# Attention and two feed-forward blocks on one core: the last product by quarters, PSUM by single banks, a new order of attention

## The chip, the cores and the metric

One core of a Trainium2 chip runs the whole program. The metric is the device time of one execution in microseconds (us), the median of several. The engines are TensorE (PE), VectorE (DVE), ScalarE (ACT), GpSimd (POOL) and SyncE (SP, which issues most DMAs); each takes its own instructions in the program's order.

## The reference

```python
# q, k, v: (2, 12, 448, 64), causal attention
scores = scale * q @ k.T                     # masked above the diagonal
attn = exp(scores - max); attn /= attn.sum() + 1e-9
x = (attn @ v)                               # (896, 768), tokens x heads*64
h = x @ w_in                                 # w_in (768, 2048)
y = (relu(h) ** 2) @ w_out                   # (896, 768)
z = maximum(maximum(y @ w1, y @ w2), y @ w3) # each w (768, 768)
out = z @ moe2_w_out                         # (896, 768)
```

## The kernel before

Everything is held transposed (features on partitions, tokens along the free axis), 448 tokens (one batch) to a matmul. Weights arrive in double precision: `Weight` (L131) loads raw words (L143), and DVE and ACT decode them in steps `clip`, `scale`, `shift`, `join`, `sign`, then split them into a high part (ACT, `act_hi`, L125) and a low part (DVE, `dve_lo`, L128). Activations are split likewise, and each product is three matmuls: high x high, high x low, low x high (`group`, L328).

**Attention** handles 12 pairs of heads. The steps of a pair are scores (`s`, L226, PE), masked minimum (`m`, L237, DVE), exponential (`e`, L246, ACT), reciprocal (`r`, DVE), normalising (`n`, L258, POOL), transposes (`g`, L266, PE), placing them in SBUF (`h`, L290, DVE for group 0, else ACT), weighted sums with v (`w`, L299, PE), and the split of the result (`xh` on ACT, `xl` on DVE). The hand-written list `ORDER` (L23) gives the order of all steps, `s4.0` being scores 4 of pair 0; each engine keeps that order. q and k of pair i + 3 are loaded at `s0.i`, v of pair i + 2 at `w0.i`. Decoding of the first `w_in` blocks (`wload`, `wc` to `wl`) and the product of block 0 for the first batch (`p0.f0` to `gl.f0`) stand in the list too. Eight warm-up matmuls of 448 columns on a zero operand come first (L446 to L449). PSUM is a pool `psa`: four `sc` banks, three `pt`, one `pv`.

**The main loop** starts when that pool is closed and pool `psb` (four accumulators of two banks, one bank for each batch) takes its place. The rounds of `front` (L489: block 1, the second batch's half of block 0, then blocks 2 to 15) make 36 matmuls each (18 for the half), with relu (L363), square (L366) and split; then `w_out` (L497, 18 rounds), then the stage with w1, w2 and w3 (L517): for each of six blocks f three rounds, copy to `m`, two maxima (L527), split into `zh` and `zl`. `decode` (L421) does, in one round, the low part of the weight two places ahead in the line of weights and all other steps of the one three places ahead, with the evacuation of the round in between; block f of the last weight (`wo`) stands behind w1, w2, w3 of f in that line.

**The last product** (L535) goes over seven row tiles of 128 tokens: 36 matmuls of 384 columns each (six f, three parts, two halves; the seventh tile is cut 480 and 288), then ACT copies the first half, DVE the second (L557, L559), and SP sends the tile out.

Of the kernel before, what the change touches and what calls it, by code (L numbers as in the profile page):

```python
# [15 lines left out]
WARM = 8  # L16
PR, PT, SC, VP = 2, 3, 4, 1
# [6 lines left out]
wload.f0 wload.f1 s4.0 m4.0 m5.0 e4.0 e5.0 s6.0 m6.0 e6.0 s2.0 m2.0 m3.0 e2.0 e3.0 r0.0 n6.0 n5.0  # L24
n4.0 s0.0 m0.0 m1.0 e0.0 e1.0 s4.1 m4.1 m5.1 e4.1 e5.1 r1.0 n3.0 n2.0 s6.1 m6.1 e6.1 r2.0 n1.0
n0.0 g3.0 h3.0 s2.1 m2.1 m3.1 e2.1 e3.1 g0.0 h0.0 r0.1 n6.1 n5.1 n4.1 s0.1 m0.1 m1.1 e0.1 e1.1
s4.2 r1.1 n3.1 n2.1 g1.0 h1.0 r2.1 n1.1 n0.1 g2.0 h2.0 m4.2 m5.2 e4.2 e5.2 g3.1 h3.1 s6.2 m6.2
e6.2 g0.1 h0.1 s2.2 m2.2 m3.2 e2.2 e3.2 r0.2 n6.2 n5.2 n4.2 w0.0 w1.0 w2.0 w3.0 xh.0 s0.2 m0.2
m1.2 e0.2 e1.2 xl.0 s4.3 g1.1 h1.1 g2.1 h2.1 m4.3 m5.3 e4.3 e5.3 r1.2 n3.2 n2.2 r2.2 n1.2 n0.2
s6.3 m6.3 e6.3 g3.2 h3.2 g0.2 h0.2 s2.3 m2.3 m3.3 e2.3 e3.3 w0.1 w1.1 w2.1 w3.1 xh.1 r0.3 n6.3  # L30
n5.3 n4.3 s0.3 m0.3 m1.3 e0.3 e1.3 xl.1 s4.4 r1.3 n3.3 n2.3 g1.2 h1.2 g2.2 h2.2 m4.4 m5.4 e4.4
e5.4 r2.3 n1.3 n0.3 g3.3 h3.3 s6.4 m6.4 e6.4 g0.3 h0.3 s2.4 m2.4 m3.4 e2.4 e3.4 r0.4 n6.4 n5.4
n4.4 w0.2 w1.2 w2.2 w3.2 xh.2 s0.4 m0.4 m1.4 e0.4 e1.4 xl.2 s4.5 g1.3 h1.3 g2.3 h2.3 m4.5 m5.5
e4.5 e5.5 r1.4 n3.4 n2.4 s6.5 m6.5 e6.5 r2.4 n1.4 n0.4 g3.4 h3.4 g0.4 h0.4 s2.5 m2.5 m3.5 e2.5
e3.5 r0.5 n6.5 n5.5 n4.5 w0.3 w1.3 w2.3 w3.3 xh.3 s0.5 m0.5 m1.5 e0.5 e1.5 xl.3 s4.6 r1.5 n3.5
n2.5 g1.4 h1.4 r2.5 n1.5 n0.5 g2.4 h2.4 m4.6 m5.6 e4.6 e5.6 g3.5 h3.5 s6.6 m6.6 e6.6 g0.5 h0.5
s2.6 m2.6 m3.6 e2.6 e3.6 r0.6 n6.6 n5.6 n4.6 w0.4 w1.4 w2.4 w3.4 xh.4 s0.6 m0.6 m1.6 e0.6 e1.6
xl.4 s4.7 g1.5 h1.5 g2.5 h2.5 m4.7 m5.7 e4.7 e5.7 r1.6 n3.6 n2.6 r2.6 n1.6 n0.6 g3.6 h3.6 s6.7
m6.7 e6.7 g0.6 h0.6 s2.7 m2.7 m3.7 e2.7 e3.7 w0.5 w1.5 w2.5 w3.5 xh.5 r0.7 n6.7 n5.7 n4.7 s0.7
m0.7 m1.7 e0.7 e1.7 xl.5 s4.8 g1.6 h1.6 r1.7 n3.7 n2.7 g2.6 h2.6 m4.8 m5.8 e4.8 e5.8 r2.7 n1.7  # L40
n0.7 g3.7 h3.7 s6.8 m6.8 e6.8 g0.7 h0.7 s2.8 m2.8 m3.8 e2.8 e3.8 w0.6 w1.6 w2.6 w3.6 xh.6 wc.f0
# [19 lines left out]
def tile_attention_moe_moe(  # L61
# [25 lines left out]
    nc = tc.nc  # L87
# [43 lines left out]
    class Weight:  # L131
# [19 lines left out]
        def clip(self):  # L151
            self.t = wp.tile(self.shape, F32, tag="wd", name="wd", bufs=2)
# [36 lines left out]


# [12 lines left out]
    class Pair:  # L203
# [124 lines left out]
    def group(acc, w, kcs, cs, x, tks, first=True, last=True):  # L328

        for a, kc in enumerate(kcs):  # L330
            wh, wl = w(kc)
            for n in range(3):
                for i, tk in enumerate(tks):
# [3 lines left out]
                        acc[:, i, :S], ww[:, cs], xx[:, tk],  # L337
# [9 lines left out]
    def moe_in(psp, w, g, bs):  # L347

        nb = len(bs)
        shape = [P, 1, 512] if psp is psa else [P, B, 512]  # L350
        acc = psp.tile(shape, F32, tag="pt" if psp is psa else "acc", name="acc", bufs=PT if psp is psa else None)
# [40 lines left out]
    front = [*range(FILL, FILL + 1), *range(FILL), *range(FILL + 1, KFF)]  # L392
# [46 lines left out]
    with tc.tile_pool(name="ga", bufs=1) as ga:  # L439
        with (  # L440
            tc.tile_pool(name="att", bufs=2) as att,
            tc.tile_pool(name="psa", bufs=2, space=bass.MemoryType.PSUM) as psa,
        ):
            prs = [att.tile([P, offs[-1]], F32, name=f"pr{n}", bufs=1) for n in range(PR)]
            warm = tp.tile([P, B, S], FR, tag="r", name="warm")
            nc.vector.memset(warm.bitcast(F32), 0.0)  # L446
            idle = psa.tile([P, S], F32, tag="pt", name="idle", bufs=PT)
            for _ in range(WARM):
                nc.tensor.matmul(idle, warm[:, 0, :P], warm[:, 1], start=True, stop=True)  # L449
# [7 lines left out]
            for f in range(FILL + EARLY):  # L457
                w = blocks_in[f]
                e = dict(
                    wload=load_next, wc=w.clip, ws=w.scale, w1=w.shift, w2=w.join, w3=w.sign, wh=w.high_part,  # L460
                    wl=w.low_part,
                )
                if f < FILL:
                    def first(f=f):
                        todo.update({
                            f"{n}.f{f}": step for n, step in
                            moe_in(psa, blocks_in[f].hl, g_tiles(ga, f, [0]), [0]).items()
                        })
# [18 lines left out]
        psb = ctx.enter_context(tc.tile_pool(name="psb", bufs=4, space=bass.MemoryType.PSUM))  # L487
        with tc.tile_pool(name="gb", bufs=1) as gb:
            for f in front:  # L489
                bs = both if f >= FILL else both[1:]  # L490
                e = moe_in(psb, blocks_in[f].hl, g_tiles(gb, f, bs), bs)
# [5 lines left out]
            for m in range(KDM):  # L497
                acc = psb.tile([P, B, 512], F32, tag="acc", name="acc")
                for n, w in enumerate(blocks_out[m]):
# [7 lines left out]
                        lambda: [act_hi(yh[b][:, m], acc[:, b, :S]) for b in range(B)],  # L507
                        lambda: [dve_lo(yl[b][:, m], acc[:, b, :S], yh[b][:, m]) for b in range(B)],
# [6 lines left out]
    zh = zp.tile([P, KF2, NT], FR, name="zh")  # L515
    zl = zp.tile([P, KF2, NT], FR, name="zl")
    for f in range(KF2):  # L517
        m = None
        for n, w in enumerate(blocks_max[f]):
            acc = psb.tile([P, B, 512], F32, tag="acc", name="acc")  # L520
            group(acc, blocks(*w.hl), range(KDM), slice(0, P), y, [every] * B)
            a = acc[:, :, :S]
            if n == 0:
                m = tp.tile([P, B, S], F32, tag="r", name="m")
                decode([lambda: nc.scalar.copy(m, a)])
                continue
# [83 lines left out]
```

## Time and profile before

| | us |
|---|---|
| median of 3 runs | 500.53 (500.27 to 500.68) |
| the profiled execution | 500.39 |
| its span, first to last instruction | 498.5 |
| busy in the span: PE, DVE, ACT, POOL | 489.9, 337.3, 212.9, 45.0 |

A row of a timeline or group names the line of the kernel, the engine, the operation, output<-inputs by the program's names with their shapes, and a count; what stands in brackets is the time for which the engine stood idle ahead of it and what ended that. PEld is TensorE's weight load, which runs beside the matmuls. Ends of matmuls are modelled, so a busy PE need not be PE at its peak.

### The profile page before, as it was taken

How to read it: one execution, taken by the hardware profiler on the slowest of the kernel's cores; microseconds unless marked ns; L12 is line 12 of the kernel's file. 1: busy time of each engine (PE TensorE's matmuls, PEld its weight loads, DVE VectorE, ACT ScalarE, POOL GpSimd, SP SyncE). 2: the span in 40 equal slices, each digit the busy share in tenths (PEclk: the TensorE clock that was granted, in tenths of full speed). 3: DMA queues.
4: the chain of work that ended last, by engine and by line, in shares of the span. 5: the costliest groups of instructions: out<-in, count | busy, mean ns of one | idle time of the engine just before them, and what ended most of it. 6: DMA issues, size and time to landing. Idle time of an engine off the chain costs nothing.

```text
span 498.5 us, 6849 instructions
## 1 busy us (share of the span) xinstructions
PE 489.9 (98%) x2612; PEld 432.7 (87%) x2612; DVE 337.3 (68%) x626; ACT 212.9 (43%) x410; POOL 45.0 (9%) x97
## 2 busy tenths in 40 slices
PE   8999998899999999999999999999999999999996
PEld 5666666899999999999999999999999999999996
DVE  4877888688877787848448457467887979852000
ACT  4999995454445445433123223233433434321000
POOL 3655554000000000000000000000000000000000
PEclk9999999999999999999999999999999999999999
DMA  8433313344324323333333243233445335300111
GB/s 297 152 123 121 124 43 83 108 128 125 95 97 128 117 75 104 126 106 121 108 110 106 81 151 121 69 126 128 136 131 177 128 126 190 126 2 32 64 63 64
DMA packets 46464, 56.28 MB, mean 113 GB/s; under 512 B 1632, under 2 KB 41824, under 8 KB 46432
## 3 DMA queue, kind: packets, MB, share of 16 engines
q1 hardware_dynamic: 46288, 55.61, 34.5%
q8 instruction: 21, 0.34, 0.3%
q10 hardware_dynamic: 144, 0.23, 0.1%
q14 instruction: 11, 0.09, 0.1%
HBM read 53.08 MB, written 2.75 MB: 112 GB/s over the span
## 4 chain that ended last, share of the span: by engine, by line
PE 97%; DVE 2%; ACT 0%; POOLq 0%; issue 0%; POOL 0%
PE acc L336 73%; PE acc L546 9%; PE sc L226 6%; PE ptp L266 4%; PE pv L299 3%; PE idle L449 1%; POOLq L606 0%; DVE wd L167 0%; DVE wd L174 0%; DVE xl L128 0%; DVE pr L237 0%; DVE wd L163 0%; DVE warm L446 0%; DVE ph L290 0%; DVE r L366 0%
## 5 line engine op out<-in xcount | busy, mean ns | idle before, releaser
L125 ACT CAST wh<-wd 128x768 fp32r<-128x768 f32 (+1 forms) x52 | 42.2, 812 | 122.7 <-DVE wd L174 122.7
L336 PE MATMUL acc<-yl,wh 128*128 128x448 f32 x216 | 61.4, 365 | 0.0
L336 PE MATMUL acc<-yh,wh 128*128 128x448 f32 x216 | 61.3, 365 | 0.0
L336 PE MATMUL acc<-yh,wl 128*128 128x448 f32 x216 | 61.3, 365 | 0.0
L336 PE MATMUL acc<-xh,wh 128*128 128x448 f32 x192 | 55.7, 366 | 1.3 <-DVE xl L128 1.3
L159 ACT ACTIVATE wd<-wd 128x768 f32<-128x768 f32 (+1 forms) x58 | 47.8, 823 | 18.8 <-DVE wd L153 18.5
L167 DVE SCALAR_TENSOR_TENSOR wd<-wr,wd 128x768 int32<-128x768 int32 (+1 forms) x58 | 54.3, 936 | 2.0
L174 DVE SCALAR_TENSOR_TENSOR wd<-wr,wd 128x768 int32<-128x768 int32 (+1 forms) x58 | 54.2, 935 | 2.0
L128 DVE TENSOR_TENSOR wl<-wd,wh 128x768 fp32r<-128x768 f32 (+1 forms) x52 | 48.1, 925 | 10.9 <-ACT wh L125 10.7
L336 PE MATMUL acc<-xl,wh 128*128 128x448 f32 x192 | 55.5, 365 | 0.0
L336 PE MATMUL acc<-xh,wl 128*128 128x448 f32 x192 | 55.5, 365 | 0.0
L336 PE MATMUL acc<-gh,wh 128*128 128x448 f32 x192 | 54.5, 365 | 0.0
L336 PE MATMUL acc<-gh,wl 128*128 128x448 f32 x192 | 54.5, 365 | 0.0
L336 PE MATMUL acc<-gl,wh 128*128 128x448 f32 x192 | 54.5, 365 | 0.0
L246 ACT ACTIVATE pr<-pr,st 128x384 f32<-128x384 f32 (+3 forms) x84 | 43.9, 527 | 6.6 <-DVE st L237 6.3
L258 POOL TENSOR_SCALAR pr<-pr,st 128x384 f32<-128x384 f32 (+3 forms) x84 | 42.6, 526 | 36.3 <-DVE st L254 11.2
L237 DVE CUSTOM_DVE_ANT_0 pr<-sc,mask 128x384 f32<-128x384 f32 (+3 forms) x84 | 34.5, 447 | 15.9 <-PE sc L226 12.3
L336 PEld LDWEIGHTS acc<-yh,wl 128*128 128x128 f32 x216 | 40.6, 188 | 3.2
L336 PEld LDWEIGHTS acc<-yh,wh 128*128 128x128 f32 x216 | 40.6, 188 | 3.2
L336 PEld LDWEIGHTS acc<-yl,wh 128*128 128x128 f32 x216 | 40.6, 188 | 3.2
L336 PEld LDWEIGHTS acc<-xh,wh 128*128 128x128 f32 x192 | 36.0, 188 | 4.2 <-DVE xl L128 1.4
L336 PEld LDWEIGHTS acc<-xh,wl 128*128 128x128 f32 x192 | 36.1, 188 | 2.9
(93 smaller groups left out, 688.1 us busy)
## 6 DMA issues: line engine op xcount, KB each, us to landing
wr<-in_moe_w_out SPq DMA_DIRECT2D x18, 768.0 KB, 4.3
wr<-in_moe_w SPq DMA_DIRECT2D x18, 768.0 KB, 4.3
wr<-in_moe_w_in SPq DMA_DIRECT2D x16, 768.0 KB, 4.7
q<-in_q SPq DMA_DIRECT2D x12, 256.0 KB, 2.7
v<-in_v SPq DMA_DIRECT2D x12, 256.0 KB, 3.6
wr<-in_moe_w_out SPq DMA_DIRECT2D x6, 512.0 KB, 3.7
k<-in_k SPq DMA_DIRECT2D x11, 224.0 KB, 2.8
out<-o SPq DMA_DIRECT2D x6, 384.0 KB, 2.3
```

The lines of the kernel that those rows point to most:

```text
L125: nc.scalar.copy(hi, src)
L128: nc.vector.tensor_tensor(out=lo, in0=src, in1=hi.bitcast(F32), op=ALU.subtract)
L159: nc.scalar.activation(self.t, self.t, ACTF.Copy, scale=2.0 ** -112)
L167: nc.vector.scalar_tensor_tensor(out=ti, in0=self.low, scalar=29, in1=ti, op0=ALU.logical_shift_right, op1=ALU.bitwise_or,)
L174: nc.vector.scalar_tensor_tensor(out=ti, in0=self.high, scalar=SIGN, in1=ti, op0=ALU.bitwise_and, op1=ALU.bitwise_or)
L226: nc.tensor.matmul(sc[:, :keys[w]], self.n["q"][r, w // 2 * P:(w // 2 + 1) * P], self.n["k"][r, :keys[w]], start=True, stop=True,)
L237: nc.vector.tensor_tensor_reduce(out=self.pr[:, offs[u]:offs[u] + n], in0=self.sc[u][:, :n], in1=mask[:, mask.shape[1] - n:], scale=-SCALE ...
L246: nc.scalar.activation(sl, sl, ACTF.Exp, bias=self.st[:, 0, u:u + 1], scale=-1.0, accum_out=self.st[:, 1, u:u + 1],)
L258: nc.gpsimd.tensor_scalar(sl, sl, self.st[:, 2, u:u + 1], 1.0, op0=ALU.mult, op1=ALU.mult)
L266: nc.tensor.transpose(pt[:, i], self.pr[:, offs[u] + kc * P:offs[u] + (kc + 1) * P], ident)
L336: nc.tensor.matmul(acc[:, i, :S], ww[:, cs], xx[:, tk], start=first and a == 0 and n == 0, stop=last and a == len(kcs) - 1 and n == 2,)
L546: nc.tensor.matmul(acc[:, i, :cols[i].stop - cols[i].start], zz[:, f, tk], ww[:, 0, cols[i]], start=f == 0 and n == 0, stop=f == KF2 - 1 a ...
```

## The change

`ORDER` is written anew: pair 0 begins with its shortest scores, loads of weights come later, decoding of blocks 0 and 1 is spread otherwise, and the whole product of block 1 (`a0` to `a5`) and the second batch of block 0 (`b0` to `b5`) stand at its end. q and k of pair 0 are loaded in two pieces each. PSUM is eight tiles of one bank, given out in turn by kind (`bank`, `one`, `next_acc`), so relu, square, maximum and copy work on one batch at a time. The warm-up is 11 matmuls of 256 columns.

The last product takes the first 768 tokens in quarters of 384 tokens x 384 inner features x 384 columns: seven products of quarters and sums of quarters, in place of eight. Sums of quarters of z (`sums_z`) and of the weight (`sums_w`) are made on DVE, in place in the unsplit values, as soon as block f is there; block 5's after the stage. Four sums of each are then split in high and low (`z_sum`, `w_sum`). On PE come first the products that need no sums (`corner`, row tile 6 in `rest`, the second half of `corner`), then, for each of three row tiles, four products, two sums, and a fifth product onto the first one's bank. Results leave in halves of 384 columns.

```diff
-WARM = 8
-PR, PT, SC, VP = 2, 3, 4, 1
+WARM = 11
+PR = 2
...
+s0.0 m0.0 m1.0 e0.0 e1.0 r2.0 n1.0 s2.0 m2.0 m3.0 e2.0 e3.0 s4.0 m4.0 m5.0 e4.0 e5.0 n0.0 s6.0
+m6.0 e6.0 r1.0 n3.0 n2.0 s0.1 m0.1 m1.1 e1.1 e0.1 s6.1 m6.1 e6.1 r0.0 n6.0 n5.0 n4.0 s4.1 m4.1
...
+w0.9 w1.9 w2.9 w3.9 xh.9 r1.11 n3.11 n2.11 g1.10 h1.10 r0.11 n6.11 n4.11 r2.11 n1.11 xl.9 n5.11
+n0.11 g2.10 h2.10 g3.10 h3.10 g3.11 h3.11 g1.11 h1.11 w1.f0 w2.f0 w3.f0 wh.f0 wl.f0 w0.10 w1.10
+w2.10 w3.10 xh.10 xl.10 ws.f1 g2.11 h2.11 g0.11 h0.11 w1.f1 w2.f1 w3.f1 wh.f1 wl.f1 p0.f0 p1.f0
+p2.f0 p3.f0 p4.f0 p5.f0 rl.f0 sq.f0 gh.f0 gl.f0 w0.11 w1.11 w2.11 w3.11 xh.11 xl.11 a0.201 a1.201
+a2.201 a3.201 a4.201 a5.201 b0.202 wload.f2 wc.f2 b1.202 b2.202 b3.202 b4.202 b5.202 ws.f2 w1.f2
+w2.f2 w3.f2 wh.f2 wl.f2
...
+    ps = [psp.tile([P, 512], F32, name=f"ps{n}") for n in range(8)]
+    def bank(kind, n):
+        own = dict(sc=range(4), pt=range(4, 7), pv=range(7, 8))[kind]
...
+    def next_acc():
+        turn["acc"] += 2
+        return [e[:, :S] for e in ps[(turn["acc"] - 2) % 8:][:2]]
...
+                cuts = (0, n) if self.i else (0, 2 * P, n)
+                for c0, c1 in zip(cuts, cuts[1:]):
+                    queue.dma_start(out=a[:, c0:c1], in_=src[self.b, self.hp][:, c0:c1])
...
+            for i in range(nb):
+                nc.scalar.activation(r[0][:, i], acc[i], ACTF.Relu)
...
+            warm = const.tile([P, 2 * P], FR, name="warm")
...
+    def sums_z(f):
+        u, v = zs[:, f, first], zs[:, f, second]
+        if f < KH:
+            each((v, u, v, ALU.subtract))
+        else:
+            a11, a21 = zs[:, f - KH, first], zs[:, f - KH, second]
+            each((v, v, a21, ALU.subtract), (a11, v, a11, ALU.add), (u, u, v, ALU.subtract))
...
+            if i == 0:
+                decode([lambda: [nc.scalar.copy(m[:, b], acc[b]) for b in range(B)]])
+                if f:
+                    sums_w(f - 1)
+                continue
...
+        if f < KF2 - 1:
+            decode([None, lambda: sums_z(f)])
+    decode()
...
+    corner = [one()[:, :n] for _ in range(TH)]
+    for t in range(TH):
+        product(corner[t], [whole(f, t, left) for f in range(KH)])
...
+    for t in range(TH):
+        nc.scalar.copy(kept[t], corner[t])
+    sums_z(KF2 - 1)
+    sums_w(KF2 - 1)
+    rest = [one()[:, :n] for _ in range(2)]
+    for f in range(KF2):
+        for acc, cs in zip(rest, (left, right)):
+            product(acc, [whole(f, NTT - 1, cs)], f == 0, f == KF2 - 1)
+    for t in range(TH):
+        product(corner[t], [whole(f, t, left) for f in range(KH, KF2)], False, more=True)
...
+    s3, t3 = z_sum(0, second, halves[0]), w_sum(0, right, pieces[:3])
+    s2, t2 = z_sum(KH, second, halves[1]), w_sum(KH, right, pieces[3:6])
+    s1, t1 = z_sum(0, first, halves[2]), w_sum(0, left, pieces[6:9])
+    s4, t4 = z_sum(KH, first, halves[3]), w_sum(KH, left, pieces[9:])
...
+    ways = iter((early * (TH + 2))[:TH + 2] + late * TH)
+    def way_out(t, cs, acc, other=None):
+        o = next(ways)
+        if other is None:
+            nc.scalar.copy(o, acc)
+        else:
+            nc.vector.tensor_tensor(out=o, in0=acc, in1=other, op=ALU.add)
+        nc.sync.dma_start(out=out[rows(t), cs], in_=o)
+    for acc, cs in zip(rest, (left, right)):
+        way_out(NTT - 1, cs, acc)
+    for t in range(TH):
+        way_out(t, left, corner[t])
+    for t in range(TH):
+        u, v = kept[t], kept[TH]
+        acc = [one()[:, :n] for _ in range(4)]
+        for a, (x, w) in zip(acc, ((s3, t3), (s2, t2), (s1, t1), (s4, w22))):
+            product(a, quarter(x, w, t))
+        for o, a, b in ((u, acc[1], u), (v, acc[2], u)):
+            nc.vector.tensor_tensor(out=o, in0=a, in1=b, op=ALU.add)
+        way_out(TH + t, right, acc[0], v)
+        product(acc[0], quarter(z22, t4, t), False, more=True)
+        way_out(t, right, acc[3], v)
+        way_out(TH + t, left, acc[0], u)
```

## Rows read from the trace of the kernel before

**Rows 1.** The page: busy time, share of the span, instructions of TensorE.
```profile
PE 489.9 (98%) x2612; PEld 432.7 (87%) x2612; DVE 337.3 (68%) x626; ACT 212.9 (43%) x410; POOL 45.0 (9%) x97
```

**Rows 2.** The chain in order of time: start us, us, what.
```profile
17.48 1.88 PE pv L299 x16
...
67.35 1.88 PE pv L299 x16
...
89.40 361.42 PE acc L336 x1782
450.82 43.77 PE acc L546 x252
...
494.61 0.57 ACT o L559
...
495.20 0.46 DVE o L557
```

**Rows 3.** Windows: stretch, length, busy us by engine, PE clock, DMA share, GB/s.
```profile
17.48:67.35 49.87, 49.87 (x371) 31.57 (x372) 38.78 (x179) 48.50 (x157) 26.56 (x55) 1.00 0.34 113
...
406.00:428.00 22.00, 22.00 (x111) 20.39 (x110) 18.42 (x23) 8.17 (x10) 0.00 (x0) 1.00 0.42 145
450.80:494.60 43.80, 43.77 (x253) 43.01 (x251) 5.54 (x8) 3.83 (x7) 0.00 (x0) 1.00 0.14 55
```

**Rows 4.** Timeline of the start: start us, us, engine, line, operation, idle before.
```profile
0.99 0.81 DVE L446 MEMSET warm<- 128x896 f32 x1 [0.99 <-PEq L576]
...
1.85 3.36 PE L449 MATMUL idle<-warm 128*128 128x448 f32 x8 [1.85 <-DVE warm L446]
...
6.94 0.56 DVE L237 CUSTOM_DVE_ANT_0 pr<-sc,mask 128x384 f32<-128x384 f32 x1 [5.14 <-PE sc L226]
```

**Rows 5.** Line 449, then line 226 in 5.1-6.95 and 6.95-8.5: min/median/max ns.
```profile
L449 PE MATMUL idle<-warm x8: 575/575/742, 1.9 to 4.6; 128*128 128x448 f32 x8
...
L226 PE MATMUL sc<-k,q x5: 832/844/1007, 5.1 to 6.7; 64*128 64x384 f32 x4, 128*128 128x448 f32 x1
...
L226 PE MATMUL sc<-k,q x7: 269/480/832, 6.7 to 8.4; 64*128 64x256 f32 x4, 128*128 128x448 f32 x2, 64*128 64x128 f32 x1
```

**Rows 6.** Timeline, PE at pairs 10 and 11 and at the main loop.
```profile
77.70 0.66 PE L266 MATMUL ptp<-ident,pr 128*128 128x128 f32 x4 [0.55 <-ACT ph L290]
...
79.08 1.95 PE L299 MATMUL pv<-ph,v 128*64 128x448 f32 x16 [0.72 <-issue]
...
81.23 1.35 PE L266 MATMUL ptp<-ident,pr 128*128 128x128 f32 x8 [0.20 <-POOL pr L258]
...
89.40 0.67 PE L336 MATMUL acc<-xh,wh 128*128 128x448 f32 x2 [1.29 <-DVE xl L128]
```

**Rows 7.** Timeline of block 4 in the w1-w2-w3 stage: DVE and PE's weight loads.
```profile
420.90 0.96 DVE L128 TENSOR_TENSOR wo4l<-wd,wo4h 128x768 fp32r<-128x768 f32 x1 [0.38 <-ACT wo4h L125]
...
426.22 0.96 DVE L128 TENSOR_TENSOR wl<-wd,wh 128x768 fp32r<-128x768 f32 x1 [0.43 <-ACT wh L125]
...
429.38 0.40 PEld L336 LDWEIGHTS acc<-yh,wl 128*128 128x128 f32 x2
```

**Rows 8.** Timeline around the start of the last product.
```profile
452.96 1.09 DVE L128 TENSOR_TENSOR zl<-m,zh 128x896 fp32r<-128x896 f32 x1 [1.01 <-ACT zh L125]
...
457.12 0.48 ACT L559 COPY o<-acc 128x384 f32<-128x384 f32 x1 [4.20 <-PE acc L546]
...
457.63 0.56 DVE L557 COPY o<-acc 128x384 f32<-128x384 f32 x1 [3.58 <-ACT o L559]
```

**Rows 9.** Groups by line: count, busy us, mean ns, idle before.
```profile
L128 DVE TENSOR_TENSOR yl<-acc,yh 128x448 fp32r<-128x448 f32 x12 | 6.9, 620 | 35.5 <-ACT yh L125 35.5
```

**Rows 10.** DMA issues: count, KB each, us to landing.
```profile
out<-o SPq DMA_DIRECT2D x6, 384.0 KB, 2.3
...
k<-in_k ACTq DMA_DIRECT2D x1, 224.0 KB, 3.6
out<-o SPq DMA_DIRECT2D x1, 144.0 KB, 1.9
```

More of the change, by code (lines that the diff above doesn't have):

```diff
@@ L30 @@
[L30 to L41, printed above, removed]
@@ L514, in tile_attention_moe_moe, with each @@
         w.pool = zp
-    zh = zp.tile([P, KF2, NT], FR, name="zh")
-    zl = zp.tile([P, KF2, NT], FR, name="zl")
+    KH, TH, n = KF2 // 2, NTT // 2, DM // 2
+    zs = zp.tile([P, KF2, NT], F32, name="zs")
+    first, second, left, right = slice(0, TH * P), slice(TH * P, 2 * TH * P), slice(0, n), slice(n, DM)
+    z1 = [zp.tile([P, KH, NT - TH * P], FR, name=f"z1{e}") for e in "hl"]
+    z2 = [zp.tile([P, KH, NT], FR, name=f"z2{e}") for e in "hl"]
+    def each(*steps):
+        for o, a, b, op in steps:
+            nc.vector.tensor_tensor(out=o, in0=a, in1=b, op=op)
@@ new lines, in tile_attention_moe_moe, with rows, whole, product @@
+            decode(evac)
+        if f < KF2 - 1:
+            decode([None, lambda: sums_z(f)])
+    decode()
+    def rows(t):
+        return slice(t * P, (t + 1) * P)
+    def whole(f, t, cs):
+        z, t = (z2, t) if f >= KH else (z1, t if t < TH else t - TH)
+        return [(e[:, f % KH, rows(t)], w[:, 0, cs]) for e, w in zip(z, blocks_o[f].hl)]
+    def product(acc, parts, start=True, stop=True, more=False):
+        for a, ((xh_, wh_), (xl_, wl_)) in enumerate(parts):
+            for i, (x, w) in enumerate(((xh_, wh_), (xh_, wl_), (xl_, wh_))):
@@ L562, in tile_attention_moe_moe @@
-        if t < NTT - 1:
-            nc.sync.dma_start(out=out[tk, :], in_=o)
+                    acc, x, w, start=start and a == 0 and i == 0,
+                    stop=stop and a == len(parts) - 1 and i == 2, skip_group_check=more,
+                )
+    corner = [one()[:, :n] for _ in range(TH)]
+    for t in range(TH):
+        product(corner[t], [whole(f, t, left) for f in range(KH)])
+    kept = [
+        tp.tile([P, 2, n], F32, tag="r", name="kept", padded_shape=[P, B, S]) for _ in range(2)
+    ]
@@ new lines, in hi_lo, with z_sum, w_sum, quarter @@
+    def hi_lo(hi, lo, src):
+        act_hi(hi, src)
+        dve_lo(lo, src, hi)
+    def z_sum(k0, tk, tl):
+        hl = tl[:, :KH], tl[:, KH:2 * KH]
+        hi_lo(*hl, zs[:, k0:k0 + KH, tk])
+        return lambda k, t: [e[:, k, rows(t)] for e in hl]
+    def w_sum(k0, cs, tls):
+        for k, tl in enumerate(tls):
+            hi_lo(tl[:, 0], tl[:, 1], blocks_o[k0 + k].t[:, 0, cs])
+        return lambda k: [tls[k][:, e] for e in range(2)]
+    def quarter(x, w, t):
+        return [list(zip(x(k, t), w(k))) for k in range(KH)]
@@ new lines, in tile_attention_moe_moe @@
+    z22 = lambda k, t: [e[:, k, rows(TH + t)] for e in z2]
+    w22 = lambda k: [e[:, 0, right] for e in blocks_o[KH + k].hl]
+    late = [w.t[:, 0, :n] for w in blocks_o]
+    early = [wp.tile([P, n], F32, tag="wd", name="o", bufs=2, padded_shape=[P, 2 * n]) for _ in range(2)]
+    ways = iter((early * (TH + 2))[:TH + 2] + late * TH)
[3 more added lines that the diff above has]
+            nc.scalar.copy(o, acc)
+        else:
+            nc.vector.tensor_tensor(out=o, in0=acc, in1=other, op=ALU.add)
+        nc.sync.dma_start(out=out[rows(t), cs], in_=o)
```

200 lines of the change are left out of this document (105 added, 95 removed).

## The prediction

> **What bounds the kernel now.** I read the busy times first: TensorE (PE) is at 98% of the span [rows 1]. A share over the whole span hides where an engine waits, so next came the chain in order of time. From 89.40 us on it is one engine without a break: 1,782 matmuls of 448 columns in 361.42 us (0.2028 us each), then the 252 of the last product in 43.77 us (0.1737 us each), then two copies and the output transfer up to the end of the span at 498.5 [rows 2]. In the middle of attention the chain is PE too: the weighted sums of pairs 0 and 8 start at 17.48 and 67.35, eight periods of 6.23 us [rows 2], in which PE is busy 49.87 us of 49.87 and ScalarE (ACT) 48.50, while VectorE (DVE) has slack with 38.78 [rows 3]. PE work of attention is thus 12 x 6.23 = 74.8 us, and block 0 for the first batch adds 18 x 0.203 = 3.7 us: 78.5 us. PE's first score starts at 5.1 [rows 5] and the main loop at 89.40, so 84.3 - 78.5 = 5.8 us are lost: 1.5 us in gaps at pairs 10 and 11 (0.55 + 0.72 + 0.20) and 1.3 us in the wait just ahead of the main loop [rows 6]; the remaining 3.0 us lie mostly in the start-up. So time can come from three places only: less PE work, PE's gaps before 89.40, and what follows the last matmul.
>
> **Last product.** Of the 252 matmuls, 216 belong to the six row tiles that make a 768x768 square; in quarters, eight products of 27 are these 216, and seven are 189. Row tile 6 keeps its 36. 225 remain: 27 fewer x 0.1737 us [rows 2] = **-4.7 us**. The products keep 384 columns, so the rate carries over. The Trainium skill ("TensorE: Matmul & The Clock Gate", section "Back-to-back issue gap") gives columns/2.4 + 2.5 ns, as an estimate 162.5 ns here; by it the term would be -4.4 us. The measured row is higher, and I use the row.
>
> What it adds runs on DVE and ACT beside PE. In bulk there is room: DVE is busy 5.5 and ACT 3.8 of this stage's 43.8 us [rows 3]. The question is order. Take zero at the last matmul of the stage before (450.8). DVE takes the last maximum and the low part, done at 3.2 as now [rows 8], then six sums of 384 columns. No such sum is in the trace; it lies between 0.48 us (ACT's 384-column copy [rows 8]) and 0.62 us (DVE's 448-column subtraction [rows 9]); I take 0.55, by columns nearest to the latter, plus 0.04 to the next dependent one: 0.59. They end at 6.7. Then come four splits of 1,152 columns, 1.36 us each (1.09 for 896 [rows 8] plus 256 more columns at 1.05 ns, the slope from 0.62 for 448), and twelve of 384 at 0.55, each after the like on ACT: DVE ends at 6.7 + 5.4 + 6.6 = 18.7, ACT, a step ahead, at about 16. Meanwhile PE has 27 + 36 + 27 matmuls that need none of them, 15.6 us. The pairs of operands are ready at about 9.7, 12.7, 15.7, 17.1 and 18.8; PE asks for them at 15.6, 17.2, 18.8, 20.3 and 21.9. The least slack is 3.1 us, so I cost them at nothing; if DVE ran a quarter slower, that cover would be gone.
>
> Behind the last split on ACT queue five output copies, with two buffers: copy three waits for the first transfer, 1.9 to 2.3 us [rows 10], and frees its PSUM bank at about 19; the fourth product of the first row tile needs that bank at 20.3. Inside a row tile DVE has two dependent sums of 0.56 (as its 384-column copy [rows 8]) between the third product's end and the reuse of the first product's bank, with nine matmuls (1.56 us) to hide them: barely covered. I add **+0.2 us** (0 to 0.9) over three row tiles.
>
> **The stage with w1, w2, w3.** New on DVE's queue are the early sums: two for each of blocks 0 to 2, six for blocks 3 and 4. A maximum becomes two of 0.62 against one of 1.09 [rows 8, 9], at most 0.15 more. The critical point is block 3's sums, which run during block 4's rounds, where DVE is already busy 18.42 us of 22 [rows 3]. Queued behind them is the low part that is now done at 427.18 and that PE's weight load asks for at 429.38, 2.2 us later [rows 7]. Six sums are 6 x 0.59 = 3.5 us; a 0.38 us wait for ACT ahead of wo4's low part [rows 7] is absorbed; net 3.1 us. PE waits 3.1 - 2.2 = **+0.9 us**, once (0 to 1.7). Two sums fit. Block 4's six come when little decoding is left; block 5's are in the last product's sum.
>
> **Start and end of attention.** The warm-up operand shrinks from 896 columns to 256: the 0.81 us memset [rows 4] becomes 0.2 to 0.8. The warm-up goes from 8 x 448 = 3,584 columns in 3.36 us [rows 4] to 11 x 256 = 2,816, about 2.6 us, so it can end near 4.0 instead of 5.2. k of pair 0 lands by 0.73 + 3.6 = 4.3 us [rows 10] in one piece; its first half, now a transfer of its own, is no later. First score: 4.1, **1.0 us** earlier. The extra q issue stands on SP's queue ahead of pair 1's k, the extra k issue on ACT, idle then; both are short and nothing early waits behind them. The two loads of w_in leave SP's queue ahead of the pairs and are first needed near pair 8, so they cost nothing there. The first scores have 128 keys, not 384, so DVE's first minimum, now at 6.94 behind slow 384-column matmuls [rows 4, 5], can start near 4.7. DVE, ACT and GpSimd fill 2 us sooner, but PE's work stays, so I take only **0.5** of the 3.0 us.
>
> At the end, accumulators come from single banks, so the main loop no longer waits for the whole attention pool and for the low part (xl) that is late now: the **1.3 us** wait [rows 6] goes. By the new order PE has, from the last groups of transposes to the main loop, 24 transposes (about 3 us), two weighted sums of 1.88 us [rows 2] and block 0's 3.7 us: 10.4 us. DVE has two decodings there, each of three operations no longer than a low part, 0.96 us [rows 7], ACT's high part between (about 0.95, twice the 384-column copy [rows 8]) and the low part itself, then xl and a copy: about 10.5, nearly level. I take half of the 1.5 us at pairs 10 and 11, **0.8 us**. Together **-3.6 us**. Ends: -1.3 (only the pool's wait goes) and -5.9 (nearly every gap goes and the start's 1.0 comes on top). The products of blocks 1 and 0, moved to the end of attention, and the splitting of relu and square are the same work under a full PE: nothing, unless PE stood still there.
>
> **The end.** Now ACT's 0.57 and DVE's 0.46 us copies follow the last matmul one after the other [rows 2], then a transfer. After: one DVE sum of 0.56 and a transfer of about that size. **-0.5 us** (0.2 to 0.6).
>
> **Sum.** -3.6 + 0.9 - 4.7 + 0.2 - 0.5 = -7.7 us on the profiled execution's 500.39 (span 498.5), that is 492.7; it lies 0.14 under the median of the runs, so the median becomes 492.8.
>
> **Rivals.** (a) The sums are late: PE waits in the last product for the bank behind the output buffers. For: ACT's queue is in order, and the slack at that bank is 1.3 us. Against: splits and other banks have 3 us or more. If one transfer and copy, some 2.8 us, shows up: 495.6. (b) The new order gains nothing before the main loop, because ACT, busy 48.50 of 49.87 us [rows 3], gives back each gap closed as PE's supplier: 492.8 + 3.6 = 496.4. Against: the 1.3 us wait has a cause that goes. (c) Slower: PE's clock. The clock column reads 1.00 throughout [rows 3]; yet the eight warm-up matmuls start from 1.9 to 4.6, 0.39 us apart against 0.203 later, and the first 384-column scores take 844 ns until about 6.7, while of the next seven, longer and shorter ones, the median is 480 [rows 5]: that is the lower of the two levels, 1.2 GHz. A shorter warm-up and small first scores that wait for DVE could leave PE at it longer. Each us of present work done at half speed costs one more, so above 9 us of it the gains are gone: if the first two pairs' 12.5 us stayed slow, 492.8 + 12.5 = 505.3. Against: PE's work starts 0.5 us earlier and is about as dense. The same page of the Trainium skill ("What's actually happening") says that activity releases the throttled default; by that the level rises about when it does now.
>
> **How the numbers follow.** Forecast 0.72, (a) 0.10, (b) 0.12, (c) 0.03, and 0.03 for (a) with (b) and a little more, near 500, which is within 0.2% (about 1.0 us, what a measurement of this kernel can tell from no change). Ends of the forecast's terms: -5.9 - 4.7 - 0.6 = -11.2, 489.3; and -1.3 + 1.7 - 4.7 + 0.9 - 0.2 = -3.6, 496.9, which takes in (a) and (b) alone. Faster 0.94, same 0.03, slower 0.03.
>
> **What would show it.** 225 matmuls after the w1-w2-w3 stage in about 39 us with no PE gap above 0.3 us; one PE gap of about a us at block 5's first round; a first DVE minimum near 4.7; the main loop's first matmul at 85.8 (83.5 to 88.1); under 3.6 us after the last matmul. Wrong would be: PE gaps behind ACT's copies (a), a main loop at 89 with ACT full (b), scores of 844 ns far beyond 7 us (c).

## The result and the profile after

The changed kernel takes **492.87 us** (median of four runs, 492.65 to 493.08) against 500.40 before (four runs, 500.02 to 500.68), a ratio of 0.985 with a 95% interval of 0.9833 to 0.9867. The profiled execution took 493.08 us with a span of 491.3; before it was 500.39 with 498.5, so the span lost 7.2 us. (Beside the experiments, the kernel before took 506 to 508 us in 16 of 33 runs and 499.5 to 500.8 in the others; no kernel with the change rose by as much, no trace shows why, and below all kernels are compared with the changed one.)

The page, and then the chain in order of time (start us, us, what), of the kernel after:

```profile
PE 485.2 (99%) x2588; PEld 429.0 (87%) x2588; DVE 363.9 (74%) x704; ACT 221.9 (45%) x451; POOL 45.1 (9%) x97
```

```profile
15.18 1.88 PE ps L329 x16
...
86.86 361.92 PE ps L366 x1782
448.77 39.11 PE ps L624 x225
487.90 0.56 DVE wd L692
```

Against [rows 2] the first weighted sum starts 2.3 us earlier, the main loop at 86.86 instead of 89.40, the 1,782 matmuls take 0.5 us more, and the last product is 225 matmuls in 39.11 us instead of 252 in 43.77. After the last matmul comes one sum on DVE and a transfer: 3.42 us to the end of the span where it was 3.91. The four terms are -2.6 (first matmul of the loop in the timelines: 89.40 to 86.78), +0.57 (from there to the last product), -4.66 and -0.49: -7.2 us.

The window of the last product (stretch, length, busy us by engine, PE clock, DMA share, GB/s), against [rows 3]:

```profile
448.80:487.90 39.10, 39.07 (x225) 38.74 (x223) 23.72 (x39) 13.65 (x25) 0.00 (x0) 1.00 0.17 62
```

DVE works 23.7 us instead of 5.5 and ACT 13.7 instead of 3.8, and PE still has no gap. The timeline (start us, us, engine, line, operation; in brackets the idle time before and what ended it) has the start, the end of attention and the one wait of the later stages:

```profile
4.78 0.29 DVE L267 CUSTOM_DVE_ANT_0 pr<-ps,mask 128x128 f32<-128x128 f32 x1 [3.65 <-PE ps L256]
...
76.72 1.09 PE L296 MATMUL ps<-ident,pr 128*128 128x128 f32 x8 [0.41 <-POOL pr L288]
...
80.22 1.09 PE L296 MATMUL ps<-ident,pr 128*128 128x128 f32 x8 [0.53 <-POOL pr L288]
...
410.13 1.62 DVE L562 TENSOR_TENSOR zs<-zs 128x384 f32<-128x384 f32 x3
...
418.50 1.74 DVE L562 TENSOR_TENSOR wd<-wd 128x384 f32<-128x384 f32 x3
...
426.00 0.96 DVE L129 TENSOR_TENSOR wl<-wd,wh 128x768 fp32r<-128x768 f32 x1 [0.43 <-ACT wh L126]
...
427.01 0.30 PEld L366 LDWEIGHTS ps<-yh,wl 128*128 128x128 f32 x2 [0.26 <-DVE wl L129]
```

The three gaps of [rows 6] are two, both waits for GpSimd's weightings (the normalising steps `n`); the wait ahead of the main loop is gone. In the stage with w1, w2, w3, PE's weight load waits once, 0.26 us, for a low part that six sums had made late.

### The profile page after: what moved, and what is told of

The parts are those of the page before. It is cut to its first block, busy times and chain, and to the rows that moved or that the text cites. A ratio compares the mean times of both kernels' runs of the same rounds, so it can differ in the third digit from the quotient of the medians.

```text
span 491.3 us, 6889 instructions
## 1 busy us (share of the span) xinstructions
PE 485.2 (99%) x2588; PEld 429.0 (87%) x2588; DVE 363.9 (74%) x704; ACT 221.9 (45%) x451; POOL 45.1 (9%) x97
## 4 chain that ended last, share of the span: by engine, by line
PE 96%; ACT 2%; POOL 1%; DVE 1%; issue 0%; POOLq 0%; DVEq 0%
PE ps L366 74%; PE ps L624 8%; PE ps L256 5%; PE ps L296 4%; PE ps L329 3%; ACT pr L276 1%; POOL pr L288 1%; PE ps L474 1%; DVE pr L267 0%; ACT wd L163 0%; POOLq L752 0%; DVE ph L320 0%; DVE wd L692 0%; ACT xh L126 0%; DVE st L283 0%
## 5 line engine op out<-in xcount | busy, mean ns | idle before, releaser
L366 PE MATMUL ps<-yh,wl 128*128 128x448 f32 x216 | 61.5, 366 | 0.0
L366 PE MATMUL ps<-yl,wh 128*128 128x448 f32 x216 | 61.5, 366 | 0.0
L366 PE MATMUL ps<-yh,wh 128*128 128x448 f32 x216 | 61.4, 366 | 0.0
L171 DVE SCALAR_TENSOR_TENSOR wd<-wr,wd 128x768 int32<-128x768 int32 (+1 forms) x58 | 54.3, 936 | 2.0
L366 PE MATMUL ps<-xh,wh 128*128 128x448 f32 x192 | 55.7, 366 | 0.0
L178 DVE SCALAR_TENSOR_TENSOR wd<-wr,wd 128x768 int32<-128x768 int32 (+1 forms) x58 | 54.0, 931 | 2.0
L366 PE MATMUL ps<-xl,wh 128*128 128x448 f32 x192 | 55.5, 365 | 0.0
L366 PE MATMUL ps<-xh,wl 128*128 128x448 f32 x192 | 55.5, 365 | 0.0
L366 PE MATMUL ps<-gl,wh 128*128 128x448 f32 x192 | 54.5, 365 | 0.0
L366 PE MATMUL ps<-gh,wh 128*128 128x448 f32 x192 | 54.5, 365 | 0.0
L366 PE MATMUL ps<-gh,wl 128*128 128x448 f32 x192 | 54.5, 365 | 0.0
L276 ACT ACTIVATE pr<-pr,st 128x128 f32<-128x128 f32 (+3 forms) x84 | 43.8, 524 | 6.2 <-DVE st L267 6.1
```

What stands on the lines that cost most here:

```text
L171: nc.vector.scalar_tensor_tensor(out=ti, in0=self.low, scalar=29, in1=ti, op0=ALU.logical_shift_right, op1=ALU.bitwise_or,)
L178: nc.vector.scalar_tensor_tensor(out=ti, in0=self.high, scalar=SIGN, in1=ti, op0=ALU.bitwise_and, op1=ALU.bitwise_or)
L276: nc.scalar.activation(sl, sl, ACTF.Exp, bias=self.st[:, 0, u:u + 1], scale=-1.0, accum_out=self.st[:, 1, u:u + 1],)
L366: nc.tensor.matmul(acc[i], ww[:, cs], xx[:, tk], start=first and a == 0 and n == 0, stop=last and a == len(kcs) - 1 and n == 2,)
```

## The experiments

Every kernel here computes the whole result; nothing is left out. Main loop and last product are named by the start of their first matmul in the timeline; the chain has it up to 0.1 us later. The 1,782 matmuls of the chain are all from the one to the other; what the expectations call "stage" is the last 648 of them, those with w1, w2 and w3. Runs of one kernel can differ by some tenths of a us, as the ranges show, so that differences of this size are read from the traces; a time without a range is of a single run.

### Which part of the new attention brings the 2.6 us

The first run gives back the wait alone (accumulators of the main loop's first round are the bank of the last weighted sum), the second gives the old list of steps, with the new products at its end.

```diff
-                ("a", "201", 1, both, next_acc), ...
+                ("a", "201", 1, both, lambda: next_acc() and [ps[7][:, :S], ps[0][:, :S]]), ...
```

> The changed kernel, but block 1's accumulators are the pv bank and bank 0, so that its first matmul has to wait until xl of pair 11 has read pv, as it had to before. Theory (single banks took a wait away): xl of pair 11 ends at about 89.0 us in the changed kernel, so the main loop starts at 89.0 instead of 86.8 and the time is 2.2 us longer, 495.1. Rival (the new order alone brought the gain, the wait was hidden): the main loop stays within 0.4 us of 86.8, 492.9 to 493.3.

```diff
-s0.0 m0.0 m1.0 e0.0 e1.0 r2.0 n1.0 s2.0 m2.0 m3.0 e2.0 e3.0 s4.0 m4.0 m5.0 e4.0 e5.0 n0.0 s6.0
...
+wload.f0 wload.f1 s4.0 m4.0 m5.0 e4.0 e5.0 s6.0 m6.0 e6.0 s2.0 m2.0 m3.0 e2.0 e3.0 r0.0 n6.0 n5.0
...
+xl.11 a0.201 a1.201 a2.201 a3.201 a4.201 a5.201 b0.202 b1.202 b2.202 b3.202 b4.202 b5.202
...
```

> The changed kernel with the old order of attention (block 1's and 0's products added behind it), all else as changed. Theory (about half of the gain ahead of the main loop is the wait, half the order): the main loop starts at 88.1, where pair 11's weighted sum ended before, less up to 0.5 for the earlier first score, so 87.6 to 88.1 and 493.7 to 494.2. Rival (the order is all of it): 89.0 or later, 495.1 or more. Rival (the order is nothing, the banks are all): 86.8, 492.9.

PE's timeline, of the first and then of the second:

```profile
89.06 0.67 PE L366 MATMUL ps<-xh,wh 128*128 128x448 f32 x2 [2.20 <-DVE xl L129]
```

```profile
4.07 4.11 PE L256 MATMUL ps<-k,q 64*128 64x384 f32 x11 [0.17 <-DMA k<-in_k]
...
77.24 0.66 PE L296 MATMUL ps<-ident,pr 128*128 128x128 f32 x4 [0.58 <-POOL pr L288]
78.63 1.95 PE L329 MATMUL ps<-ph,v 128*64 128x448 f32 x16 [0.73 <-issue]
80.78 1.35 PE L296 MATMUL ps<-ident,pr 128*128 128x128 f32 x8 [0.20 <-POOL pr L288]
...
87.58 0.67 PE L366 MATMUL ps<-xh,wh 128*128 128x448 f32 x2
```

With the wait given back the loop starts at 89.06: it costs 2.3 us and eats nearly all of the gain. With the old list it starts at 87.58, and the three gaps of [rows 6] stand as they were. The four cases of the main loop's start are 89.40 (old list, wait), 89.06 (new list, wait), 87.58 (old list, no wait) and 86.78 (new list, no wait). The first of them is the kernel before, which has the old warm-up and loads too: in the run with the old list the first score comes at 4.07 instead of 5.14, and of the 1.8 us between 89.40 and 87.58 the wait is 1.3, which leaves 0.5 for this earlier start. The new list with the wait would have won 0.3 us: PE, earlier at the end of attention, waits that much longer for the same low part, 2.20 us for 1.29. The runs of these two kernels scatter, 494.97 to 496.87 and 492.74 to 496.04 us; the profiled ones, from which the starts are, took 494.97 and 493.46. By the medians, 496.49 and 493.80, they lose 3.6 and 0.9 us to the changed kernel, by the starts 2.3 and 0.8; what lengthened three of the four runs with the wait further stays open.

### Is the last product worth 4.66 us, and are the early sums needed for it

First the old last product in the changed kernel, without any sums, then the seven products with every sum made after the stage.

```diff
-    corner = [one()[:, :n] for _ in range(TH)]
...
+    for t in range(NTT):
+        tk = slice(t * P, (t + 1) * P)
...
+        for f, i in order if t < NTT - 1 else sorted(order, key=lambda e: e[1]):
+            part(f, i)
...
```

> The changed kernel with the last product as before: eight products, 252 matmuls, no sums. Theory (27 matmuls are worth 4.7 us, and the sums cost PE only the 0.6 us that the w1-w2-w3 stage grew by): last product 43.8 us, stage 131.3 us between first matmuls, time 492.9 + 4.7 - 0.6 = 497.0. Rival (the sums cost more than that elsewhere): below 496.3.

```diff
-                if f:
-                    sums_w(f - 1)
...
-            decode([None, lambda: sums_z(f)])
+            decode()
...
-    sums_z(KF2 - 1)
-    sums_w(KF2 - 1)
+    for f in range(KF2):
+        sums_z(f)
+        sums_w(f)
```

> The changed kernel with all sums of z and of the weight made after the w1-w2-w3 stage. Theory (the sums are hidden only because they are early): 18 more sums of about 0.56 us stand ahead of the splits on DVE, so the operands of the first product with sums come at about 19.3 us instead of 9.2 after the stage, and PE asks at 15.6: PE waits some 3.6 us there and 1 to 2 more behind it, while the 0.6 us in the stage go; 496.9 to 498.3. Rival (DVE has room in the last product, so it does not matter when they are made): 492.3.

The chain of the first and its ACT copy of the last tile's first half; then the waits (engine, line, waited for: us in total, times, longest us) and a window of the second:

```profile
86.87 361.34 PE ps L366 x1782
448.21 43.77 PE ps L585 x252
...
489.65 0.56 ACT L594 COPY o<-ps 128x480 f32<-128x480 f32 x1 [3.94 <-PE ps L585]
```

```profile
PE ps L622 <- DVE wsums L129: 2.3, 2, 1.4
PE ps L622 <- DVE wd L691: 1.4, 1, 1.4
...
464.00:476.00 12.00, 7.21 (x36) 5.92 (x35) 11.86 (x19) 8.10 (x17) 0.00 (x0) 1.00 0.18 66
```

The old last product took 496.89 us (496.89 to 496.93), as expected: 43.77 us for 252 matmuls, and 361.34 for the 1,782. Against its profiled 496.93 the changed kernel's 493.08 is 3.85 us less, not 4.66: the stage with w1, w2 and w3 gives back 0.57 and the end 0.3. For with an accumulator of its own in a single bank the first half of the last tile is copied at 489.65, ahead of the last matmul, and only 3.1 us follow that matmul (3.42 in the changed kernel, 3.91 before). With all sums late the time was 498.83 us, a little above the range given. From 464 to 476 DVE is busy 11.9 of 12 us and PE only 7.2: DVE, with the sums and the splits queued behind them, became the bound. Without the early sums seven products are slower than eight, by 498.83 - 496.89 = 1.9 us; the early sums are what makes the seven pay.

### The wait in the stage with w1, w2, w3

The sums of block 3's weights are made a block later, with block 4's.

```diff
-                if f:
-                    sums_w(f - 1)
+                for e in ((), (0,), (1,), (2,), (), (3, 4))[f]:
+                    sums_w(e)
```

> The changed kernel with the weight sums of block 3 made one block later, together with block 4's. Theory (PE's one wait in the w1-w2-w3 stage is for the low part queued behind six sums): three sums fewer ahead of it let that low part come 1.2 to 1.6 us earlier, PE does not wait, the stage takes 131.35 us between first matmuls as without sums, and the last product stays at 39.1; 492.3 to 492.7. Rival (DVE is simply full in these rounds): the wait comes back a round later, 492.9 or more.

```profile
86.88 361.35 PE ps L366 x1782
448.23 39.10 PE ps L624 x225
```

Measured: 492.58 us (492.55 to 492.62), no wait of PE's weight load, and the last product as fast as before. The sums queued ahead of that low part are the cause, and a block later they cost nothing that the trace shows.

### The start

First without warm-up, then with the reciprocals of pair 0's first scores queued two minima later.

```diff
-WARM = 11
+WARM = 0
```

> The changed kernel with no warm-up matmuls. Theory (PE's rate doubles only after it has worked for a while, so rival (c) of the prediction has a price, and the shorter warm-up just suffices): scores run at the lower rate for 2 us or more longer, and the main loop starts at 88.0 to 90.8 instead of 86.8. Rival (in the start-up PE waits for DVE anyway, so its rate there does not matter): 86.8 within 0.4 us.

```diff
-s0.0 m0.0 m1.0 e0.0 e1.0 r2.0 n1.0 s2.0 m2.0 m3.0 e2.0 e3.0 s4.0
+s0.0 m0.0 m1.0 e0.0 e1.0 s2.0 m2.0 m3.0 r2.0 n1.0 e2.0 e3.0 s4.0
```

> The changed kernel with the reciprocals of the first two minima (r2.0, n1.0) moved behind the next two minima in ORDER. Theory (the start-up lost as much as before because DVE stands waiting for the first exponentials, 0.73 us at 6.0, while two minima are ready): DVE and with it PE's first transposes come 0.4 to 0.7 us earlier, and the main loop starts at 86.1 to 86.5. Rival (GpSimd's first normalisings, now later, set it): 86.8 or later.

The groups of PE's first 10 us (count, busy us, mean ns), of the kernel after, then of the one without warm-up, then of the one with block 3's sums later, whose start is that of the kernel after:

```profile
L256 PE MATMUL ps<-k,q 128*128 128x448 f32 x4 | 2.0, 591 | 0.5 <-DVE st L267 0.5
L256 PE MATMUL ps<-k,q 64*128 64x384 f32 x8 | 1.9, 523 | 0.0
```

```profile
L256 PE MATMUL ps<-k,q 128*128 128x448 f32 x4 | 2.9, 813 | 0.0
L256 PE MATMUL ps<-k,q 64*128 64x384 f32 x6 | 2.3, 790 | 0.0
```

```profile
L256 PE MATMUL ps<-k,q 64*128 64x384 f32 x8 | 2.5, 689 | 0.0
```

Without warm-up the scores stay long, as those of [rows 5] at the lower clock level, while the clock column reads 1.00 in both; yet the first transposes come only 0.7 us later (10.72 against 10.02), the main loop 0.4 (87.19), and the time was 493.49 us. DVE and ACT set the pace there, so PE's slowness is mostly hidden. The third kernel shows the same without any edit at the start: its 384-column scores take 689 ns, not 523, and yet its first transposes start at 10.02 and its main loop at 86.81, as in the kernel after. In the second run DVE's next minima no longer stand behind the reciprocal of pair 0's first scores: the first transposes start at 9.80, the main loop at 86.28, 0.5 us earlier, and the time was 492.55 us.

### What holds the two gaps at the end of attention

Three runs, each following what the one before suggested. First, ACT's scaling of block 0 behind the exponentials it stood ahead of:

```diff
-... xh.8 ws.f0 s2.11 ... n0.10 e6.11 g0.10
+... xh.8 s2.11 ... n0.10 e6.11 ws.f0 g0.10
```

> The changed kernel with one step of block 0's decoding on ACT (ws.f0) moved behind the last exponential. Theory (at pairs 10 and 11 PE waits for GpSimd, and GpSimd for exponentials that stand behind this step on ACT): GpSimd's last run starts 0.7 us earlier, PE's waits of 0.41 and 0.53 us shrink by 0.5 to 0.9 in sum, the main loop starts at 85.9 to 86.3. Rival (DVE's decoding of block 0, which needs that step, is late instead): 86.8 or later.

```profile
73.63 6.51 POOL L288 TENSOR_SCALAR pr<-pr,st 128x256 f32<-128x256 f32 x10 [2.77 <-DVE st L284]
```

A miss: 493.08 us, main loop 86.75, gaps 0.41 and 0.58. GpSimd's last run of ten weightings still starts late, after 2.77 us idle behind a reciprocal. The next run feeds it earlier:

```diff
-r0.10 n6.10 n5.10 n4.10 g0.9 ... e3.11 xl.8 s4.11 m4.11 m5.11 e4.11 e5.11 r1.10 n3.10 n2.10 s6.11 m6.11 n0.10 e6.11
+r0.10 n6.10 n5.10 n4.10 n0.10 g0.9 ... e3.11 xl.8 r1.10 n3.10 n2.10 s4.11 m4.11 m5.11 e4.11 e5.11 r1.11 n3.11 n2.11 s6.11 m6.11 e6.11
-xh.9 r1.11 n3.11 n2.11 g1.10
+xh.9 g1.10
```

> One weighting of pair 10 (n0) moved into GpSimd's 2.8 us of idle time ahead of its last run, and the reciprocals r1 of pairs 10 and 11 moved ahead of the next minima on VectorE, nothing else. Theory (the last run of ten weightings is late because it starts late, on a reciprocal queued behind three minima, and carries one weighting that could have run before): the run starts at about 72.6 instead of 73.7, holds nine and ends at 78.6 to 79.2 instead of 80.17; both TensorE gaps (0.41 and 0.53) go, main loop from 85.8 to 86.0, time 491.9 to 492.2. Rival (it ends when the last exponentials and their reciprocals allow, whatever stands ahead): the run ends above 79.8, main loop 86.5 to 86.8, time 492.5 to 493.1.

```profile
72.77 0.93 POOL L288 TENSOR_SCALAR pr<-pr,st 128x256 f32<-128x256 f32 x2 [1.48 <-ACT pr L276]
74.11 0.93 POOL L288 TENSOR_SCALAR pr<-pr,st 128x256 f32<-128x256 f32 x2 [0.42 <-DVE st L284]
75.83 4.17 POOL L288 TENSOR_SCALAR pr<-pr,st 128x448 f32<-128x448 f32 x5 [0.78 <-DVE st L283]
```

The weightings start 0.9 us earlier and yet end at 80.00 instead of 80.17, as the rival had it: main loop 86.59, 492.55 us. The last five begin at 75.83, when the last reciprocals are there, and take 4.17 us; by their like elsewhere (0.64 for 448 columns, 0.58 for 384, 0.37 for 128) it should be 0.64 + 2 x 0.58 + 2 x 0.37 = 2.5. Three operations on DVE that decode block 0 run in the same stretch. The last run moves those to earlier idle times of DVE, in the kernel with all edits that is given below.

```diff
-xh.7 xl.7 ... e6.10 r0.10 ... s2.10 m2.10 ... xh.8 ws.f0 s2.11 ... h1.11 w1.f0 w2.f0 w3.f0 wh.f0 wl.f0
+ws.f0 xh.7 xl.7 w1.f0 ... e6.10 w2.f0 r0.10 ... s2.10 w3.f0 m2.10 ... xh.8 s2.11 ... h1.11 wh.f0 wl.f0
```

> The run with all three edits, and besides the bit operations that decode the first block of weights (one scaling on ScalarE, three 128x768 integer operations on VectorE) moved from beside GpSimd's last run of weightings to earlier idle times of VectorE; nothing is left out. In the runs so far a weighting of 384 columns takes 0.58 us alone and 0.88 to 1.28 while one of these integer operations runs, one of 128 columns 0.37 alone and 1.06; the operations too are longer (1.22 against 0.96). Theory (the two engines hold each other up there, and that is why GpSimd's last run ends at 80 us whatever stands ahead of it): the last five weightings take 2.5 to 2.7 us instead of 4.17 and end by 78.6, the gap of 0.56 before the last transposes goes, main loop from 85.4 to 85.7 instead of 86.12, time 491.1 to 491.5 against 491.83 of the profiled run without. Rival (the weightings are long for another reason, or the last reciprocals come late by as much as is won): the run ends above 79.3, main loop 86.0 to 86.5, time 491.7 to 492.5.

Groups of GpSimd's last weightings by size (count, busy us, mean ns) and timeline of DVE's operations and of PE's scores; first of the kernel that has the decoding beside the weightings, then of the one that has not:

```profile
L288 POOL TENSOR_SCALAR pr<-pr,st 128x384 f32<-128x384 f32 x2 | 2.2, 1096 | 0.0
L288 POOL TENSOR_SCALAR pr<-pr,st 128x128 f32<-128x128 f32 x2 | 1.4, 716 | 0.0
...
69.76 2.30 PE L256 MATMUL ps<-k,q 64*128 64x256 f32 x10
...
76.45 1.22 DVE L171 SCALAR_TENSOR_TENSOR wd<-wr,wd 128x768 int32<-128x768 int32 x1
```

```profile
L288 POOL TENSOR_SCALAR pr<-pr,st 128x384 f32<-128x384 f32 x2 | 1.2, 586 | 0.0
L288 POOL TENSOR_SCALAR pr<-pr,st 128x128 f32<-128x128 f32 x2 | 0.7, 372 | 0.0
...
66.75 0.95 DVE L171 SCALAR_TENSOR_TENSOR wd<-wr,wd 128x768 int32<-128x768 int32 x1
...
68.68 1.14 DVE L178 SCALAR_TENSOR_TENSOR wd<-wr,wd 128x768 int32<-128x768 int32 x1
...
69.48 2.94 PE L256 MATMUL ps<-k,q 64*128 64x256 f32 x10
...
75.90 2.45 POOL L288 TENSOR_SCALAR pr<-pr,st 128x448 f32<-128x448 f32 x5 [0.78 <-DVE st L283]
```

The two engines do hold each other up: the five take 2.45 us alone and 4.17 beside the decoding, and DVE's operation of L171 0.95 against 1.22. The gap of 0.56 us before the last transposes is gone. But the time is not won: the main loop starts at 86.05 instead of 86.12. The third operation (L178) now stands ahead of four minima, banks for scores come free later, and PE's ten scores there take 2.94 instead of 2.30 us; the other gap grew from 0.20 to 0.39, and that operation now doubles a weighting of 384 columns at 69.00 (1.28 us). The mechanism was right, the price of its removal elsewhere as high.

The rows of the kernel before already had this: three weightings (448, 384 and 384 columns) took 1.77 us at 69.08 and the same three 2.76 at 74.88, beside the same decoding.

```profile
69.08 1.77 POOL L258 TENSOR_SCALAR pr<-pr,st 128x448 f32<-128x448 f32 x3 [0.83 <-ACT pr L246]
...
74.88 2.76 POOL L258 TENSOR_SCALAR pr<-pr,st 128x448 f32<-128x448 f32 x3 [2.01 <-DVE st L237]
```

### Versions that beat the changed kernel

The later reciprocals at the start with the later sums of block 3 (first); the same with GpSimd's earlier weightings (second).

> Both gains at once: the reciprocals and the first weighting of pair 0 behind the two next minima (0.50 us earlier main loop when alone), and block 3's sums of weights with block 4's (no wait of TensorE in the stage, 0.5 us shorter when alone). If the two are independent: main loop from 86.3, stage of 131.3 to 131.4, last product 39.1, time 491.9 to 492.3. If the wait in the stage depends on when the stage starts and comes back elsewhere: 492.5 or more.

> The edits of the two other runs together. If all three gains are independent: main loop from 85.3 to 85.5, stage 131.3 to 131.4, last product 39.1, time 490.9 to 491.4. If the gain of the weightings is none: as the run without them, 491.9 to 492.3.

The chain of the first, then of the second:

```profile
86.39 361.35 PE ps L366 x1782
447.74 39.13 PE ps L624 x225
```

```profile
86.19 361.34 PE ps L366 x1782
447.53 39.08 PE ps L624 x225
```

The first takes 492.14 us (491.69 to 492.73), the second 492.12 (491.83 to 492.48), and the kernel with the early decoding 491.94 (491.77 to 492.04). By their medians all three beat 492.87, by 0.7 to 0.9 us, though the slowest run of the first (492.73) lies above the fastest of the changed kernel (492.65); between the three the runs don't decide. The chain of the first has both gains, 0.47 us at the main loop and 0.57 behind it; the second's 0.2 us of main loop (its expectation of 85.3 to 85.5 missed) is within the spread of the runs.

## Why the prediction was right, and where its steps were not

The forecast was 492.8 us and the median 492.87; the likeliest case held and no rival came. On the profiled execution the terms summed to -7.7 us and the span lost 7.2. By its own terms:

**Last product: -4.7 + 0.2, measured -4.66.** 27 matmuls fewer at the old rate: 39.11 / 225 = 0.1738 us each. By the estimate of 162.5 ns after the Trainium skill ("TensorE: Matmul & The Clock Gate", section "Back-to-back issue gap"), whose formula that section calls the isolated gap of a single matmul, the term would have been -4.4; the trace does not agree, and the row was the better price. The reuse of banks inside a row tile, priced at +0.2, cost nothing: PE has no gap in the stage. Rival (a) did not come: ACT's copies waited 1.68 and 1.52 us for output transfers, as it had them, and PE was not reached. What the prediction took for granted, room for the sums, is only there because most are made earlier: the run with late sums took 5.8 us more than the profiled 493.08.

**Stage with w1, w2, w3: +0.9, measured +0.57.** Place and cause were right, the make-up was not. Six sums took 1.62 + 1.74 = 3.36 us (0.54 to 0.58 each, not 0.59), and DVE's idle times absorbed 0.9 of it, not 0.4; the wait was 0.26 us. That explains less than half of the 0.57. The rest is a slower rhythm of the matmuls behind the wait, which the prediction didn't have (last section).

**Start and end of attention: -3.6, measured -2.6.** Here sizes failed. The -3.6 were 1.0 for the earlier first score, 0.5 of the start-up loss, 1.3 for the wait and 0.8 at pairs 10 and 11. The wait went wholly (1.29). The step "I take half of the 1.5 us at pairs 10 and 11" gave 1.47 - 0.94 = 0.5: it weighed decoding on DVE against PE's work ("nearly level"), but both gaps that are left are waits for GpSimd's weightings, which stood in no term, and which the decoding itself slows, as a row of before could have told. That leaves 2.62 - 1.29 - 0.53 = 0.8 us for the start, where 1.5 were forecast. The first score did come 1.3 us earlier (3.83) and the first minimum at 4.78 (forecast 4.7), so the failed step is "I take only 0.5 of the 3.0 us": the start-up loss did not shrink, it grew by 0.5 (by subtraction). The run with the old list lost as much: first score 1.07 us earlier, 0.5 of it at the main loop. The two runs on the start agree: a slower PE there costs 0.4 us only, while one reciprocal placed later wins 0.5. It is the order on DVE, ACT and GpSimd that limits the start; the forecast let these engines "fill 2 us sooner" by the earlier first score alone.

**The end: -0.5, measured -0.49.** One sum of 0.56 us and a transfer, as forecast. But the quarters did not bring this: with the old last product and single banks the end was 0.8 shorter than before, since ACT's copy no longer stands between the last matmul and DVE's copy.

**Rivals (b) and (c).** ACT did not give everything back, though it is nearly full ahead of the two gaps that are left: 9.99 of 11 us (the row has the stretch and its length, then PE, PEld, DVE, ACT and POOL).

```profile
64.00:75.00 11.00, 11.00 (x78) 6.54 (x78) 8.37 (x35) 9.99 (x32) 3.88 (x8) 1.00 0.19 49
```

The clock was a small matter: without any warm-up, and with scores at 813 ns, the time rose by 0.4 us against a run of 493.08. The reason is not that the clock rises early but that PE waits for the other engines there anyway. (By the forecast's own -7.7 us the gains of (c) would be gone above 7.7 us at half speed, not above 9.)

The terms missed by +1.0, -0.3 and -0.2 us; that the sum missed by 0.5 only is partly luck.

## What to carry to other kernels

Fewer matmuls paid here only because most of the work that replaces them is done before the stage that needs it; look in the stages ahead for idle time of the same engine, and place it where no weight is asked for soon after. Before the wait at a stage's border is priced, ask how much longer it would grow if all ahead of it came earlier: here the same wait was 1.3 us with the old list and 2.2 with the new. Where a queue's last run seems late, compare the duration of each instruction with its like elsewhere before moving what stands ahead of it.

## What the runs showed of the hardware that was not expected

**Behind a single late weight the matmuls can run slower.** In the runs with the wait for the late low part the 1,782 matmuls take either 361.5 us (361.49 to 361.56, three kernels) or 361.9 (361.91 or 361.92, four kernels, the changed one among them); in five without it 361.34 or 361.35. So the wait itself costs about 0.2 us, and in the slower kind 0.4 more come from somewhere. Two sixes of matmuls behind it, in the timeline of the kernel after and then of the one with earlier weightings alone, which had the same wait of 0.26 us:

```profile
439.93 0.57 PE L366 MATMUL ps<-yh,wh 128*128 128x448 f32 x2
...
441.17 0.57 PE L366 MATMUL ps<-yh,wh 128*128 128x448 f32 x2
...
442.41 0.57 PE L366 MATMUL ps<-yh,wh 128*128 128x448 f32 x2
```

```profile
440.69 0.57 PE L366 MATMUL ps<-yh,wh 128*128 128x448 f32 x2
...
441.91 0.57 PE L366 MATMUL ps<-yh,wh 128*128 128x448 f32 x2
```

Six matmuls take 1.24 us in the one and 1.22 in the other, up to the end of the stage: over the 21.8 us from 427.0 to 448.8 that is 17 x 0.02 = 0.35 us. That the wait brings on the slower kind is argued, not shown: no run without the wait has it, and of the seven with the wait three have not. What decides between the two kinds stays open; that the changed kernel's runs near 493.07 and near 492.65 are these two was not shown.

**GpSimd and DVE stall each other.** A weighting of 128 columns took 0.37 us alone and 1.06 beside DVE's operation with two inputs in SBUF, one of 384 columns 0.58 and up to 1.28. The Trainium skill ("GPSIMD Engine Reference", section "Specifications") lists this contention, with DVE instructions that have two SBUF inputs or run in a two-port mode; the trace agrees for two inputs. A minimum of 384 columns, with one of its inputs in PSUM, took 0.55 us with GpSimd idle and beside a weighting.
